# Expert 1 by seven products of halves, and its rows turned while unit 0's second layer runs

## The chip, the cores and the metric

The kernel runs on one core of a Trainium2 chip. The metric is the time of one execution in microseconds (us) of device time; a profiled execution has, beside its own time, a span from the first instruction to the last.

## What is computed

A linear attention over 4 batches, 8 heads and 576 positions feeds a dense block of three input matrices with a maximum over them, and this feeds a layer of eight experts, of which each of the 2304 tokens uses two. Cut to what matters here:

```
def _moe_ref(x, w1, w2, w3, w_out):
    h = np.maximum(np.maximum(x @ w1, x @ w2), x @ w3)
    return h @ w_out                                   # 512 -> 768 -> 512

def _moe2_ref(x, w_gate, w_noise, noise, w1, w2):
    noisy_logits = x @ w_gate + np.log1p(np.exp(x @ w_noise)) * noise
    top2 = np.argpartition(-noisy_logits, 2, axis=1)[:, :2]
    ...
    for e in range(E):                                 # 8 experts, 512 -> 1024 -> 512
        for k in range(2):
            mask = top2[:, k] == e
            h = np.maximum(x[mask] @ w1[e], 0.0)
            out[mask] += top2_w[mask, k, None] * (h @ w2[e])
```

Inputs and outputs are float32.

## The kernel before

Every float32 matrix is split into a high part in the matmul's own format and the low rest (`split`: an ACT copy and a DVE subtraction), and a product is three matmuls: high by high, high by low, low by high. The program is one list of steps with planned times (`at`, `pe`, `after`); sorted by these times it is the order on PE, ACT, DVE and SP. POOL's DMAs and additions keep the order of the list too where `in_order` stands. Each engine works through its own instructions in order, and so does SP's queue of DMAs.

After the attention (some 180 us) the dense block works through six chunks of 384 tokens (`first`, `larger`, `hidden`, `second`). While it runs, DVE, ACT, POOL and SP do side work: the routing of finished chunks, which scatters each token's row into a table `meta` in DRAM by its expert, and the sum jobs (`quarter_load`, `quarter_sum`, `quarter_high`, `quarter_out`), which prepare sums and differences of quarters of the experts' first matrix and write their high and low parts to `sums`.

Then come the expert units: unit 0 is expert 0 with up to 512 rows, unit 1 the next 128 rows of expert 0, and units 2 to 8 are experts 1 to 7 with up to 608 rows each. In unit 0 and in unit 2 the first layer is done plainly (`expert1`): 8 blocks of hidden features, 4 blocks of input features, 3 matmuls, and for 608 rows two halves of 304 columns, that is 192 matmuls in unit 2. From unit 3 on (`seven(n)`, n > SEVEN = 2) it is done by seven products of halves (`product`, `sum7`, `relu7`, `low7`): seven matrix products of half the size in every direction in place of eight, 168 matmuls of 304 columns, with additions of results on DVE. The operands of the rows, named B11, B21, T1 to T4 and B22, are made by `x_quarters` and `x_sums` from the turned rows; those of the weights are either plain quarters (kind "A") or come from `sums` (kind "S").

The rows of a unit are fetched by token number: `load_meta` loads the table, `gather_x` fetches 128 rows by an indirect DMA of POOL, `turn_x` turns them by four transposes of PE into a PSUM bank t. The second layer (`expert2`, 24 matmuls of 512 columns for 128 rows) ends in `expert_out`: DVE multiplies by the gate and adds the old output that `gather_prev` had read, and an indirect DMA of POOL scatters the result. Unit 1 has its rows as the stationary operand (`tile1`), turns its hidden tile (`tile_turn`) and splits it (`tile_hidden`).

A ring of 12 slots holds weights; slot i+12 is loaded when the weights of slot i have been used (`refill`: `w2_load` by SP into a buffer `raw`, `w2_high` on ACT, `w2_low` on DVE; for kind "S" `w2_high` is two DMAs straight from `sums`). PSUM banks are s0 to s2, t0 and t1, and p0, p1 and k in turn (`bank_acc`).

In unit 0 the turn of unit 1's rows stands ahead of the last of the four tiles of the second layer; the five turns of unit 2's rows stand in unit 1:

```
                if n == 0 and i == len(sizes(M)) - 1:
                    pe(0.45, turn_x, 1, cap_b, 0)
                pe(d2, expert2, n, e, M, i)
```

Of the kernel before, what the change touches and what calls it, by code (L numbers as in the profile page):

```python
# [38 lines left out]
def tile_linear_attention__then__moe__then__noisy_top2_moe(  # L39
# [59 lines left out]
    SEVEN = 2  # L99
# [1001 lines left out]
    def gather_x(n, M, i, nrow, slot=None):  # L1101
        m = sizes(M)[i]
        xgs = st["xgs"]
        if seven(n):
            if len(st["xg7"]) == 1:
                st["xg7"].append(pools["po"].tile([P, DM], F32R, name="xg"))
            xgs, slot = st["xg7"], i % 2
# [6 lines left out]
    def turn_x(n, M, i):  # L1114
# [8 lines left out]
        xh, xl = st["gx"]  # L1123
        cs = slice(i * P, i * P + m)
# [122 lines left out]
    def tile1(n, e, a):  # L1247
        xh, xl = st["gx"]
        p_ = bank_s()
        i = 0  # L1250
        for d in range(KD):
            wh, wl = (w[:, a * HALF2:(a + 1) * HALF2] for w in WE[e, d])
            for l, r in ((xh, wh), (xh, wl), (xl, wh)):
                nc.tensor.matmul(p_, l[:, d, :P], r, start=(i == 0), stop=(i == 3 * KD - 1))
                i += 1
# [342 lines left out]
    def refill(i, n, wait=0.1, rooms=True):  # L1598
        for i in range(i, i + n):
# [4 lines left out]
            if summed(*pairs[i]):  # L1604
                if rooms:
                    after(wait + 1.0 + 3.0 * (i % 4), w2_high, *pairs[i])
                continue
            en, j = pairs[i]
            slow = n_now[0] > 1
            t = max(clock[0] + wait, split_at[-1] + (4.5 if slow else 3.0))  # L1610
            at(max(split_at[-2] + 0.01, t - 9.0), w2_load, en, en, j)
# [66 lines left out]
    for n, (e, M, row0) in enumerate(units):  # L1678
# [35 lines left out]
        else:  # L1714
            for a in range(2):
                pe(2.56, tile1, n, e, a)
                after(0.0, tile_relu, n, a)
# [6 lines left out]
        elif n:  # L1724
            refill(base(e), KD, 3.0 if n == 1 else 0.1)
# [11 lines left out]
        if n == 0:  # L1737
# [3 lines left out]
            at(tp + 17.1, gather_x, 1, cap_b, 0, N + 1, 4)  # L1741
            for i in range(4):
                at(tp + 20.0, gather_x, 2, cap, i, N + 1)
        elif n == 1:
            for i in range(4, nt2):
                at(g0, gather_x, 2, cap, i, N + 1)
        elif nxt:
# [3 lines left out]
        d2 = 3 * F2 * DM / 2400  # L1751
        if M <= P:

            pe(0.45, tile_turn, n, 0)
            after(0.0, tile_hidden, n, 0)
            pe(0.45, turn_x, n + 1, M2, 0)
            pe(0.45, tile_turn, n, 1)
            after(0.0, tile_hidden, n, 1)
            pe(0.45, turn_x, n + 1, M2, 1)
            for a in range(2):  # L1760
                pe(d2 / 2, expert2, n, e, M, 0, range(a * F2 // 2, (a + 1) * F2 // 2))
# [98 lines left out]
```

## Time and profile before

| | |
|---|---|
| median of 3 runs | 944.88 us (944.87 to 945.2) |
| profiled execution: time, span | 945.21 us, 943.7 us |
| PE busy | 930.9 us, 6841 matmuls |
| DVE, ACT, POOL busy | 592.6, 479.0, 512.4 us |
| granted TensorE clock, mean | 0.999 |

The span lies 1.5 us under the execution's own time. Matmuls overlap in their pipeline, so the length of a stretch of PE is read from the start of its first matmul to the start of what follows.

### The profile page before, as it was taken

The page shows a single profiled execution, that of the slowest core. Times are in us where ns is not written, and L with a number is a line of the kernel's source. Part 1 is how long each engine was busy: PE and PEld are TensorE (multiplying, and loading weights), DVE is VectorE, ACT ScalarE, POOL GpSimd, SP SyncE. Part 2 cuts the span into 40 slices and gives each one's busy share as a digit, 9 for nine tenths or more (in the row PEclk, how much of TensorE's full clock was granted, in tenths as well). Part 3 has the DMA queues.
Part 4 walks back from the last instruction along what each step waited for, and adds up shares of the span by engine and source line. Part 5 has one row for each costly group of instructions (what it writes and reads, how often), then busy time and mean ns, then how long its engine had stood idle before and what let it go on. Part 6 is the DMA issues. An engine that isn't in the chain of part 4 may idle for free. (4 is left out here: it accounts for less than half of the span.)

```text
span 943.7 us, 18315 instructions
## 1 busy us (share of the span) xinstructions
PE 930.9 (99%) x6841; PEld 809.3 (86%) x6841; DVE 592.6 (63%) x1251; ACT 479.0 (51%) x1021; POOL 512.4 (54%) x570
## 2 busy tenths in 40 slices
PE   8999999999999999999999999999999999999997
PEld 7777777899999999999997889798987989898895
DVE  6999999895544637363464354566685767657541
ACT  6999998554333333343343243355463735545340
POOL 6888898454474745544243532365564636556262
PEclk9999999999999999999999999999999999999999
DMA  7676653541567566656053646457565757648312
GB/s 196 164 221 178 181 181 108 190 150 59 163 172 235 169 222 178 214 183 206 4 179 112 173 131 259 173 174 276 159 254 173 278 163 235 222 149 310 92 34 73
DMA packets 121580, 164.95 MB, mean 175 GB/s; under 512 B 35438, under 2 KB 83694, under 8 KB 121490
## 3 DMA queue, kind: packets, MB, share of 16 engines
q1 hardware_dynamic: 110002, 133.83, 45.2%
q0 software_dynamic: 10928, 29.62, 9.2%
q8 instruction: 54, 0.88, 0.4%
q10 hardware_dynamic: 560, 0.33, 0.1%
q14 instruction: 36, 0.29, 0.1%
HBM read 117.28 MB, written 47.05 MB: 174 GB/s over the span
## 5 line engine op out<-in xcount | busy, mean ns | idle before, releaser
L886 PE MATMUL s<-xh,wh 128*128 128x384 f32 x432 | 148.1, 343 | 0.4 <-ACT wh L276 0.4
L886 PE MATMUL s<-xh,wl 128*128 128x384 f32 x432 | 145.4, 337 | 0.4 <-DVE wl L278 0.4
L886 PE MATMUL s<-xl,wh 128*128 128x384 f32 x432 | 145.1, 336 | 0.0
L1332 POOL DMA_INDIRECT out_dram<-o,emeta x40 | 46.8, 1170 | 125.4 <-DVE o L1330 66.5
L1407 DVE TENSOR_TENSOR wl<-raw,wh 128x1024 fp32r<-128x1024 f32 x58 | 71.2, 1227 | 30.0 <-ACT wh L1399 29.5
L896 DVE TENSOR_TENSOR a<-s,a 128x384 f32<-128x384 f32 x72 | 39.9, 554 | 77.4 <-PE s L886 76.7
L886 PEld LDWEIGHTS s<-xh,wh 128*128 128x128 f32 x432 | 81.2, 188 | 6.6 <-DVE a L896 2.2
L1322 PE MATMUL p<-wh,hh 128*128 128x512 f32 (+1 forms) x216 | 86.4, 400 | 0.0
L1322 PE MATMUL p<-wh,hl 128*128 128x512 f32 (+1 forms) x216 | 85.4, 395 | 0.0
L1322 PE MATMUL p<-wl,hh 128*128 128x512 f32 (+1 forms) x216 | 85.2, 395 | 0.0
L886 PEld LDWEIGHTS s<-xl,wh 128*128 128x128 f32 x432 | 81.2, 188 | 1.5
L886 PEld LDWEIGHTS s<-xh,wl 128*128 128x128 f32 x432 | 81.1, 188 | 0.7 <-DVE wl L278 0.7
L1399 ACT ACTIVATE wh<-raw 128x1024 fp32r<-128x1024 f32 x58 | 61.1, 1056 | 34.0 <-DMA raw<-in_moe_w_dram 19.3
L1047 POOL DMA_INDIRECT meta<-mt,si x36 | 37.0, 1028 | 52.8 <-DVE si L1043 43.6
L1375 POOL TENSOR_TENSOR raw<-raw 128x256 f32<-128x256 f32 x24 | 21.7, 903 | 75.1 <-DMA raw<-in_moe_w_dram 51.8
L1180 PE MATMUL s<-gx,wh 128*128 128x304 f32 x288 | 62.1, 303 | 0.0
L243 POOL TENSOR_TENSOR nm<-nm,bits 128x512 int32<-128x512 int32 (+1 forms) x32 | 38.3, 1206 | 42.0 <-DVE nm L233 26.1
L131 ACT ACTIVATE hh<-a 128x384 fp32r<-128x384 f32 x36 | 18.8, 522 | 80.7 <-DVE a L896 80.7
L132 DVE TENSOR_TENSOR gx<-t,gx 128x512 fp32r<-128x512 f32 (+3 forms) x82 | 39.5, 496 | 30.7 <-ACT gx L131 30.5
L131 ACT ACTIVATE gx<-t 128x512 fp32r<-128x512 f32 (+3 forms) x82 | 34.9, 448 | 42.7 <-DVE t L1155 27.4
L1109 POOL DMA_INDIRECT gx<-x2d,emeta x28 | 28.7, 1023 | 41.5 <-PE t L1119 17.1
L1330 DVE SCALAR_TENSOR_TENSOR o<-p,emeta,pv 128x512 f32<-128x512 f32 (+1 forms) x27 | 20.2, 749 | 47.3 <-PE p L1322 41.3
(318 smaller groups left out, 2642.4 us busy)
## 6 DMA issues: line engine op xcount, KB each, us to landing
raw<-in_moe_w_dram SPq DMA_DIRECT2D x58, 512.0 KB, 4.4
raw<-in_moe_w_dram SPq DMA_DIRECT2D x48, 256.0 KB, 4.0
sums<-qh SPq DMA_DIRECT2D x24, 512.0 KB, 3.0
sums<-raw SPq DMA_DIRECT2D x24, 512.0 KB, 3.4
wh<-sums SPq DMA_DIRECT2D x24, 512.0 KB, 6.1
wl<-sums SPq DMA_DIRECT2D x24, 512.0 KB, 7.0
bits<-in_moe_w_dram SPq DMA_DIRECT2D x18, 512.0 KB, 5.7
out_dram<-zrow SPq DMA_DIRECT2D x9, 512.0 KB, 3.9
```

The lines of the kernel that those rows point to most:

```text
L131: nc.scalar.activation(hi, src, AF.Copy)
L132: nc.vector.tensor_tensor(lo, src, hi.bitcast(F32), op=ALU.subtract)
L243: in_order(nc.gpsimd.tensor_tensor(m_[:, i:i + w], m_[:, i:i + w], low[:, i:i + w], op=ALU.add))
L886: nc.tensor.matmul(p_, a[:, d, fs], b_, start=(n == 0), stop=(n == 3 * KD - 1))
L896: nc.vector.tensor_tensor(a, p_, st.pop("a"), op=ALU.max)
L1047: ins = nc.gpsimd.indirect_dma_start(out=meta, out_offset=bass.IndirectOffsetOnAxis(ap=si[:, t, kk:kk + 1], axis=0), in_=mt[:, t, kk, :], ...
L1109: in_order(nc.gpsimd.indirect_dma_start(out=xg.bitcast(F32)[:m], out_offset=None, in_=x2d[0:nrow, :], in_offset=bass.IndirectOffsetOnAxis( ...
L1180: nc.tensor.matmul(bk["p"], a[:, d, fs], b_[:, d, :], start=(d == 0 and i == 0), stop=(d == 1 and i == 2))
L1322: nc.tensor.matmul(p_, a, b_[:, fw], start=(f == 0 and r == 0), stop=(f == (3 if seven(n) else F2 - 1) and r == 2))
L1332: alone(e, nc.gpsimd.indirect_dma_start(out=out, out_offset=bass.IndirectOffsetOnAxis(ap=mt[:m, i, 1:2], axis=0), in_=o[:m], in_offset=Non ...
L1399: nc.scalar.activation(WE[e, i][0], st["w2", e, i], AF.Copy)
L1407: nc.vector.tensor_tensor(wl, st.pop(("w2", e, i)), wh.bitcast(F32), op=ALU.subtract)
```

## The change

`SEVEN` becomes 1, so unit 2 (expert 1) has its first layer by seven products too, and four more sum jobs (28 in place of 24) prepare its weights, at a pitch of 7.4 planned us and not 8.0. The buffers of the gathered rows of unit 2 are then two in turn (one in the big tile, called gx in a row, one of its own, called xg), and unit 1's rows come through the second of them. Since the operands of unit 2 lie in the big tile, unit 1's operands `x1` move to two of the three buffers named pv, and its hidden tile `th` to the buffers of `o`. The turns of unit 2's rows move: the first stands ahead of the third tile of unit 0's second layer together with unit 1's turn, the second ahead of the fourth tile, the third and fourth behind it, the fifth in unit 1. In unit 1 `tile1` is cut, `tile_turn` put between its pieces, and the second layer is begun ahead of the second `tile_turn`. Times of `refill` and places of `gather_prev` change with it.

```diff
-    SEVEN = 2
+    SEVEN = 1
...
     def gather_x(n, M, i, nrow, slot=None):
...
-        if seven(n):
-            if len(st["xg7"]) == 1:
-                st["xg7"].append(pools["po"].tile([P, DM], F32R, name="xg"))
-            xgs, slot = st["xg7"], i % 2
+        if n == 1:
+            st["xg7"].append(pools["po"].tile([P, DM], F32R, name="xg"))
+        if n == 1 or seven(n):
+            xgs, slot = st["xg7"], i % 2 if seven(n) else 1
...
         xh, xl = st["gx"]
+        if n == 1:
+            st["x1"] = xh, xl = tuple(pools["po"].tile([P, KD, P], F32R, name="x1", tag="pv", bufs=3)
+                                      for _ in range(2))
...
-        h = pools["po"].tile([P, HALF2], F32, name="th", tag="pv", bufs=3)
+        h = pools["po"].tile([P, HALF2], F32, name="th", tag="o", bufs=2)
...
-                t = clock[0] + 8.0 * i
+                t = clock[0] + 7.4 * i
...
-            for a in range(2):
-                pe(2.56, tile1, n, e, a)
-                after(0.0, tile_relu, n, a)
+            pe(2.56, tile1, n, e, 0)
+            after(0.0, tile_relu, n, 0)
+            pe(1.28, tile1, n, e, 1, range(2))
+            pe(0.45, tile_turn, n, 0)
+            after(0.0, tile_hidden, n, 0)
+            pe(1.28, tile1, n, e, 1, range(2, KD))
+            after(0.0, tile_relu, n, 1)
+            after(0.01, gather_prev, 1, 0, cap_b, 0)
...
-            refill(base(e), KD, 3.0 if n == 1 else 0.1)
+            refill(base(e), KD - 1, 1.9)
...
+            pe(0.7 * 2, expert2, n, e, M, 0, range(2))
             pe(0.45, tile_turn, n, 1)
             after(0.0, tile_hidden, n, 1)
...
+            turns7(4)
+            rows7(2)
+            pe(0.7 * 2, expert2, n, e, M, 0, range(2, 4))
+            pe(d2 / 2, expert2, n, e, M, 0, range(4, F2))
             after(0.0, expert_out, n, e, M, 0)
...
-                if n == 0 and i == len(sizes(M)) - 1:
+                if n == 0 and i == 2:
                     pe(0.45, turn_x, 1, cap_b, 0)
+                    after(0.02, gather_x, 2, cap, 1, N + 1)
+                    turns7(0, 1)
+                if n == 0 and i == 3:
+                    turns7(1, 1)
+                    rows7(0)
                 pe(d2, expert2, n, e, M, i)
...
+                if n == 0 and i == 2:
+                    after(0.0, gather_prev, n, e, M, 3)
...
+        if n == 0:
+            turns7(2, 1)
+            turns7(3, 1)
+            rows7(1, 2.6)
```

On POOL, in unit 0's second layer, before: the three table loads (unit 1, unit 2 and its rest) are followed by five gathers and then by the outputs (`out_dram`) of unit 0's tiles and the reads of old output (`pv`).

```order
L1076 DMA emeta<-meta 128x3
L1076 DMA emeta<-meta 128x4x3
L1080 DMA emeta<-meta 96x3
L1109 DMA gx<-x2d,emeta 128x512 x5
L1332 DMA out_dram<-o,emeta 2304x512
L1294 TENSOR_SCALAR ic<-emeta 128x1
L1297 DMA pv<-out_dram,ic 128x512
```

With the change, from the third table load to unit 0's last output; the first xg is unit 1's gather, the others are unit 2's rows 0 to 3 in turn (gx, xg, gx, xg).

```order
L1080 DMA emeta<-meta 96x3
L1109 DMA xg<-x2d,emeta 128x512
L1109 DMA gx<-x2d,emeta 128x512
L1334 DMA out_dram<-o,emeta 2304x512 x2
L1109 DMA xg<-x2d,emeta 128x512
L1109 DMA gx<-x2d,emeta 128x512
L1334 DMA out_dram<-o,emeta 2304x512
L1296 TENSOR_SCALAR ic<-emeta 128x1
L1299 DMA pv<-out_dram,ic 128x512
L1109 DMA xg<-x2d,emeta 128x512
L1334 DMA out_dram<-o,emeta 2304x512
```

Two gathers stay ahead of the outputs, and the gather of unit 2's fourth tile (the last xg) now stands behind unit 0's third output, the index clamp and the read of the fourth tile's old output.

On PE, with the change, the end of unit 0's second tile and the start of its third (bank k):

```order
L1324 MATMUL p_6898<-wh,hl_6847 128x512
L1119 MATMUL t_6928<-exact,xg 128x128 x4
L1119 MATMUL t_6937<-exact,gx 128x128 x4
L1324 MATMUL k<-wh,hh_6598 128x512
L1324 MATMUL k<-wl,hh_6598 128x512
```

Two turns, of unit 1's rows and of unit 2's first tile, now stand here; before, PE went from the second tile to the third directly, and unit 1's turn stood ahead of the fourth.

On DVE, with the change, at the end of unit 1 and the start of expert 1: the last row pieces of unit 2 (48 columns, t_7131), a weight split (wl), unit 1's output (o from bank k) and the first additions of the seven products.

```order
L132 TENSOR_TENSOR gx<-t_7131,gx 128x4x48
L132 TENSOR_TENSOR gx<-t_7131,gx 128x2x48
L1409 TENSOR_TENSOR wl<-raw,wh 128x1024
L1158 TENSOR_TENSOR t_7131<-b_7145,t_7131 128x2x48
...
L1158 TENSOR_TENSOR t_7131<-t_7131,b_7146 128x2x48
L132 TENSOR_TENSOR gx<-t_7131,gx 128x2x48
L132 TENSOR_TENSOR gx<-b_7146,gx 128x2x48
L132 TENSOR_TENSOR gx<-t_7131,gx 128x4x48
L1332 SCALAR_TENSOR_TENSOR o<-k,emeta,pv 128x512
L1409 TENSOR_TENSOR wl<-raw,wh 128x1024
L1202 TENSOR_TENSOR u<-s_7219,t 128x304
L1202 TENSOR_TENSOR u<-k,t 128x304
```

Unit 1's output is read out of bank k behind all the row pieces, and bank k is used again by the second product of expert 1 (u from k).

## Rows read from the trace of the kernel before

**Rows 1.** The page's table of engines: busy time, share of the span, instructions.

```profile
PE 930.9 (99%) x6841; PEld 809.3 (86%) x6841; DVE 592.6 (63%) x1251; ACT 479.0 (51%) x1021; POOL 512.4 (54%) x570
```

**Rows 2.** PE busy in two stretches: first layers of experts 1 and 2.

```profile
558.69:585.65 26.96, 26.96 (x194) 1.00 0.63 224
615.28:638.83 23.55, 23.55 (x170) 1.00 0.61 203
```

**Rows 3.** Timeline of PE: start, length, instruction, idle time before it and releaser.

```profile
657.45 0.49 PE L1119 MATMUL t<-exact,gx 96*128 96x96 f32 x4 [0.20 <-DMA gx<-x2d,emeta]
...
713.45 0.49 PE L1119 MATMUL t<-exact,gx 96*128 96x96 f32 x4 [1.23 <-DMA gx<-x2d,emeta]
...
873.81 0.49 PE L1119 MATMUL t<-exact,gx 96*128 96x96 f32 x4 [0.41 <-DMA gx<-x2d,emeta]
```

**Rows 4.** Busy time of each engine from 244 to 486 us, the dense stage.

```profile
sum 242.00, PE 242.00 PEld 226.40 DVE 119.94 ACT 88.48 POOL 119.31; mean PE 48.40 PEld 45.28 DVE 23.99 ACT 17.70 POOL 23.86
```

**Rows 5.** The same from 522 to 559 us: unit 0's second layer, unit 1.

```profile
sum 37.00, PE 37.00 PEld 30.05 DVE 14.46 ACT 10.33 POOL 14.80; mean PE 18.50 PEld 15.02 DVE 7.23 ACT 5.17 POOL 7.40
```

**Rows 6.** The sum jobs' split: duration in ns (least/median/most), first and last start.

```profile
L1384 ACT ACTIVATE qh<-raw x24: 1044/1053/1065, 237.0 to 437.5; 128x1024 fp32r<-128x1024 f32 x24
...
L1389 DVE TENSOR_TENSOR raw<-raw,qh x24: 1210/1227/1762, 239.2 to 438.5; 128x1024 fp32r<-128x1024 f32 x24
```

**Rows 7.** Timeline of PE, three tiles of second layers and two turns.

```profile
533.24 0.40 PE L1322 MATMUL k<-wh,hh 128*128 128x512 f32 x1
...
538.85 0.45 PE L1119 MATMUL t<-exact,gx 128*128 128x128 f32 x4
539.13 0.47 PE L1322 MATMUL p<-wh,hh 128*128 128x512 f32 x1
...
604.13 0.48 PE L1322 MATMUL p<-wh,hh 128*128 128x512 f32 x1
```

**Rows 8.** Timeline of POOL in unit 0's second layer: table loads, two gathers.

```profile
525.44 1.38 POOL L1076 DMA_DIRECT2D emeta<-meta  x2 [3.60 <-DMA meta<-mt,si]
...
530.36 1.02 POOL L1109 DMA_INDIRECT gx<-x2d,emeta  x1 [3.00 <-DMA emeta<-meta]
531.69 1.53 POOL L1109 DMA_INDIRECT gx<-x2d,emeta  x1 [0.30 <-issue]
```

**Rows 9.** Landing times of the five gathers from 530.36, then of the second.

```profile
DMA to landing us min/median/max: 3.6/4.1/5.3
...
DMA to landing us min/median/max: 5.3/5.3/5.3
```

**Rows 10.** Timeline of SP's queue, 522 to 536 us: loads of weights.

```profile
522.32 3.08 SPq L1349 DMA_DIRECT2D raw<-in_moe_w_dram  x2
529.60 3.18 SPq L1346 DMA_DIRECT2D raw<-in_moe_w_dram  x2
```

**Rows 11.** Landing time of the gather issued at 550.23.

```profile
DMA to landing us min/median/max: 3.2/3.2/3.2
```

**Rows 12.** Landing time of the table load issued at 525.44.

```profile
DMA to landing us min/median/max: 4.6/4.6/4.6
```

**Rows 13.** Timeline of DVE: two outputs and a last low part.

```profile
533.44 0.75 DVE L1330 SCALAR_TENSOR_TENSOR o<-p,emeta,pv 128x512 f32<-128x512 f32 x1 [1.08 <-PE p L1322]
...
608.13 0.36 DVE L132 TENSOR_TENSOR gx<-t,gx 128x192 fp32r<-128x192 f32 x1 [0.23 <-ACT gx L131]
609.97 0.75 DVE L1330 SCALAR_TENSOR_TENSOR o<-p,emeta,pv 128x512 f32<-128x512 f32 x1 [1.48 <-PE p L1322]
```

**Rows 14.** Timeline of POOL: outputs, read of old output, gather.

```profile
594.65 1.03 POOL L1332 DMA_INDIRECT out_dram<-o,emeta  x1 [5.35 <-DVE o L1330]
...
596.25 1.05 POOL L1297 DMA_INDIRECT pv<-out_dram,ic  x1 [0.28 <-POOL ic L1294]
...
611.00 0.99 POOL L1332 DMA_INDIRECT out_dram<-o,emeta  x1 [3.74 <-DVE o L1330]
...
709.45 0.94 POOL L1109 DMA_INDIRECT gx<-x2d,emeta  x1 [0.30 <-issue]
```

More of the change, by code (lines that the diff above doesn't have):

```diff
@@ L1245, in tile_linear_attention__then__moe__then__noisy_top2_moe, with tile1 @@
     HALF2 = FF2 // 2
[L1247 to L1251, printed above, removed]
+    def tile1(n, e, a, ds_=range(KD)):
+        xh, xl = st["x1"] if n == 1 else st["gx"]
+        p_ = st["tp", n, a] if ds_[0] else bank_s()
+        for d in ds_:
             wh, wl = (w[:, a * HALF2:(a + 1) * HALF2] for w in WE[e, d])
-            for l, r in ((xh, wh), (xh, wl), (xl, wh)):
-                nc.tensor.matmul(p_, l[:, d, :P], r, start=(i == 0), stop=(i == 3 * KD - 1))
-                i += 1
+            for i, (l, r) in enumerate(((xh, wh), (xh, wl), (xl, wh))):
+                nc.tensor.matmul(p_, l[:, d, :P], r, start=(d == 0 and i == 0),
+                                 stop=(d == KD - 1 and i == 2))
         st["tp", n, a] = p_
     def tile_relu(n, a):
-        h = pools["po"].tile([P, HALF2], F32, name="th", tag="pv", bufs=3)
+        h = pools["po"].tile([P, HALF2], F32, name="th", tag="o", bufs=2)
         nc.scalar.activation(h, st.pop(("tp", n, a)), AF.Relu)
@@ L1605, in refill @@
                 if rooms:
-                    after(wait + 1.0 + 3.0 * (i % 4), w2_high, *pairs[i])
+                    after(0.3 + 0.6 * (i % 4) if n_now[0] == 1 else wait + 1.0 + 3.0 * (i % 4), w2_high, *pairs[i])
                 continue
             en, j = pairs[i]
-            slow = n_now[0] > 1
+            slow = n_now[0] > 0
             t = max(clock[0] + wait, split_at[-1] + (4.5 if slow else 3.0))
-            at(max(split_at[-2] + 0.01, t - 9.0), w2_load, en, en, j)
+            at(max(split_at[-2] + 0.01, t - (4.0 if n_now[0] == 1 else 9.0)), w2_load, en, en, j)
             at(t, w2_high, en, j)
@@ L1740, in tile_linear_attention__then__moe__then__noisy_top2_moe @@
                 at(tp + 17.0, load_meta, n_, row_, M_, 0)
[L1741 to L1747, printed above, removed]
+            at(tp + 17.1, gather_x, 1, cap_b, 0, N + 1)
+            at(tp + 20.0, gather_x, 2, cap, 0, N + 1)
+        elif n > 1 and nxt:
             at(g0 + 2.0, load_meta, n + 1, row2, M2, 0)
@@ L1751, in tile_linear_attention__then__moe__then__noisy_top2_moe, with turns7, rows7 @@
         d2 = 3 * F2 * DM / 2400
+        def turns7(i, n=n):
+            pe(0.45, turn_x, n + 1, cap, i)
+            if i + 2 < len(sizes(cap)):
+                after(0.02, gather_x, n + 1, cap, i + 2, N + 1)
+        def rows7(j, wait=1.6):
+            after(0.5, x_quarters, j)
+            after(wait, x_sums, j)
         if M <= P:
[L1754 to L1756 removed]
+            pe(0.7 * 2, expert2, n, e, M, 0, range(2))
             pe(0.45, tile_turn, n, 1)
             after(0.0, tile_hidden, n, 1)
[L1759 to L1763 removed]
+            turns7(4)
+            rows7(2)
+            pe(0.7 * 2, expert2, n, e, M, 0, range(2, 4))
+            pe(d2 / 2, expert2, n, e, M, 0, range(4, F2))
             after(0.0, expert_out, n, e, M, 0)
[L1765 to L1775 removed]
+        else:
             if nxt and n > 0:
@@ L1799, in tile_linear_attention__then__moe__then__noisy_top2_moe @@
                         rows7(2)
+        if n == 0:
+            turns7(2, 1)
+            turns7(3, 1)
+            rows7(1, 2.6)
         if n:
-            refill(base(e) + (len(ORDER7) if seven(n) else KD), F2 // 2, 15.0 if n == 1 else 0.1)
+            if seven(n):
+                refill(base(e) + len(ORDER7), F2 // 2)
+            else:
+                refill(base(e) + KD - 1, F2 // 2 + 1, 0.3)
     ET = mybir.EngineType
```

19 lines of the change are left out of this document (3 added, 16 removed).

## The prediction

> **What bounds the kernel now.** I read the page's table of engines first. PE is busy 930.9 of 943.7 us [rows 1], so only two things can move the time: fewer TensorE instructions, or new waits of TensorE. Then I cut the second part of the trace into stretches. The first layer of expert 1, by twelve products per output block, takes 26.96 us of PE without a gap. The first layer of expert 2, by seven products of halves, takes 23.55 us [rows 2]. The second half of the program is a chain of such stretches with few holes. Where there are holes, most stand ahead of the fifth turn of gathered rows, which waits for an indirect DMA: 0.20, 1.23 and 0.41 us [rows 3]. In the dense stage the wide jobs run under a PE that is busy 242.00 of 242.00 us [rows 4]. Unit 0's second layer and unit 1 run without a hole as well, 37.00 of 37.00 us [rows 5]. So gain and loss have to be read at two places: the first layer of expert 1, and the 37 us ahead of it, where the change puts turns that need fresh gathers.
>
> **The saving.** Expert 1 goes from 192 matmuls of 304 columns to 168, the count that experts 2 to 7 have (the counts in the rows, 194 and 170, take in a neighbour or two). By [rows 2] that is 26.96 - 23.55 = 3.4 us. The matmuls of unit 1, of both second layers and the six turns are the same in number as before, only elsewhere. I take that part as even.
>
> **Four more sum jobs in the dense stage.** Each has four POOL additions, one ACT copy of 1.05 us, one DVE subtraction of 1.23 us [rows 6] and its loads and stores; 28 jobs at a pitch of 7.4 instead of 24 at 8.0. DVE is busy 119.94, ACT 88.48 and POOL 119.31 of 242 us there [rows 4], four jobs add about 5 us to DVE and 4 to ACT. PE waits for nothing in this stage, and what hides the jobs is the PE's own work. I cost them at nothing. If a job's subtraction came straight before an evacuation that PE needs, it would cost at most its 1.2 us, once.
>
> **First wait: rows of units 1 and 2 in unit 0's second layer.** The turn of unit 1's rows stood after the third tile (at 538.85) and now stands after the second, with the first turn of expert 1 behind it. PE is there at 533.24 [rows 7]. The gathers can't come sooner than POOL lets them: the landing of the last routing scatter releases the table loads at 525.44, and the landing of the first table releases the first gather at 530.36; the second starts at 531.69 [rows 8]. The change touches neither. In before the five gathers from there took 3.6 to 5.3 us from issue to landing, the second one 5.3 [rows 9], so it landed at 537.0. The new turn of expert 1's first tile is wanted at 533.24 + 0.28 = 533.5. If nothing gets quicker, PE waits 537.1 - 533.5 = 3.6 us. But in before two loads of 512 KB were issued from 529.60 on, in this very stretch [rows 10], and these now wait for slots of unit 1. A gather in a quiet stretch landed after 3.2 us [rows 11]; the table load took 4.6 us here [rows 12]. If both took 3.2, the first gather would start at 525.44 + 3.2 + 0.3 = 528.9, the second 1.3 later, and land at 533.4: no wait. Between 0 and 3.6 I take 1.0, nearer to the quiet end, since the later loads are gone but those from 522.32 on are partly still there when the table is read.
>
> **Second wait: the fourth tile of expert 1.** This one hangs on an order and less on the state of the DMAs. Its gather stands on POOL behind unit 0's third scatter, an index clamp and the read of old output, and that scatter needs the third tile's result. Counted from the end of that tile on PE: 0.2 until DVE starts (533.24 to 533.44), 0.75 for the result, 0.28 until POOL starts (610.72 to 611.00) [rows 13, 14]; from scatter to read 1.6, the read 1.05, 0.3 between DMAs [rows 14]: 4.2 us until the gather is issued. Then 3.2 (quiet) to 5.3 us to the landing, and 0.1: 7.5 to 9.6. PE gets to the fourth turn after one turn, one tile and another turn: 0.28 + 5.6 + 0.28 = 6.2 us (a tile is 533.24 to 538.85, a turn 538.85 to 539.13) [rows 7]. So the wait is 1.3 to 3.4 us, wherever the first wait put the tile. No load of SP stands there, so I take 1.5. The same kind of chain is seen in before: the gather of 709.45 [rows 14] ends in the hole of 1.23 us.
>
> The Trainium skill, in "DMA: Bandwidth & Descriptors", section "Anatomy of one DMA — SWDGE (gpsimd) path", gives a DMA of POOL's queue about 2.0 us plus its bytes over 436 GB/s. For a gather of 256 KB that is 2.6 us, an estimate from that section of the Trainium skill, and each of the two waits would be about 0.6 us shorter by it. The rows say otherwise: none of the six gathers of [rows 9, 11] landed in less than 3.2 us.
>
> **Third wait: bank k at the start of expert 1.** The last piece of expert 1's operands (48 columns) is now made some 7 us ahead of its use, and unit 1's output comes behind it on DVE: two low parts, a weight split, four subtractions, three low parts, and only then the output from bank k. From the end of a fifth turn (604.13) [rows 7] to the last of these low parts (608.49) the same pieces took 4.4 us. A weight split on ACT and DVE, of the shapes of [rows 6], adds 1.1 and 1.15, the output 0.75 [rows 13]: 7.4 us. PE has three quarters of a tile (4.2) and three products (3 x 0.85, from 23.55 / 28) until it writes bank k again, 6.75 us. So 0.6 us of wait with the release; 0 to 1.2, as the weight split falls.
>
> **Others.** Expert 1's own fifth turn becomes one of those that wait for a gather with POOL's low parts in its queue. Of the five experts that do so in before, the one that makes the overflow table waited 1.23 us, the others 0.20, 0.41 and twice nothing: 0.1. The transposes of unit 1's hidden tile wait for an ACT step that is now among the row pieces; the second half of the tile, 1.4 us, covers it, and I give it nothing (0.5 if the cover is short). Weights of expert 1's last three products are loaded when unit 1 frees their slots, and are wanted some 14 us later; nothing, unless half-megabyte loads take three times the 4.6 us of [rows 12].
>
> **Sum.** -3.4 + 1.0 + 1.5 + 0.6 + 0.1 = -0.2 us. The profiled execution took 945.21 us, 0.3 over the median of 944.88; from the median that is 944.7. With every wait at its low end it is -3.4 + 1.3 = -2.1; with every wait at its high end -3.4 + 3.6 + 3.4 + 1.2 + 0.5 + 0.4 = +5.7.
>
> **Rivals.** A measurement tells a difference of about 0.2%, 1.9 us, from no change.
> - *The waits all but vanish (faster).* The first gather lands in time, the fourth tile's wait is at its 1.3 us or below, the third is covered: 944.88 - 2.1 to - 3.4, or 941.5 to 942.8. For it speaks that SP is idle there now; against it, that the second wait is an order of instructions. With what lies between it and 943.0 I give it 0.28. By the gather time of the Trainium skill's "DMA: Bandwidth & Descriptors" it would nearly be this case: waits of 0.4, 0.9, 0.6 and 0.1, 943.5.
> - *The turns are too early for the gathers (slower).* Table load and gathers need what they needed in before, 4.6 and 5.3 us; the first wait is 3.6 and the second 3.4. With the rest that is +4.3, or 949.2. It decides from 5.3 us of waits in all. Against it: the loads that shared the DMAs are gone. 0.12.
> - *The sum jobs show on PE (slower).* With the waits above, two subtractions of 1.2 us in front of evacuations that PE needs are enough: -0.2 + 2.4, or 947.1. PE shows no hole with 24 jobs. 0.03.
>
> The forecast, saving and waits cancelling to within 1.9 us, has 0.57.
>
> **How the numbers follow.** Forecast 944.7 us. Faster 0.28, same 0.57 and slower 0.15 come straight from the cases. The range leaves out a good tenth below, where the waits come to less than 0.8 us in all (942.3), and the slower cases above, where they come to more than 5.3 (946.8).
>
> **What would show it.** The first layer of expert 1 in some 23.5 us of PE. A hole of PE ahead of the turn of expert 1's first rows, released by the gather, of 0 to 3.6 us; one ahead of its fourth tile of 1.3 us or more; one of half a microsecond at the second pair of products, released by DVE's output from bank k. No hole in the dense stage. The prediction is wrong if the fourth tile's turn doesn't wait, or if holes of over 5 us stand between unit 0's second tile and expert 1's second layer.

## The result: 953.6 us, slower by 0.9%

The changed kernel takes 953.57 us (median of 6 runs, 951.97 to 955.6) where the kernel before takes 945.04 beside it (6 runs, 944.87 to 946.2): a ratio of 1.009, 95% interval 1.0075 to 1.0105. The forecast was 944.7 with a range up to 946.8, so the time lies outside it, 8.9 us above the forecast. The profiled execution took 955.29 us with a span of 953.4, against a span of 943.7 before. Where times of a few us are told below, it helps to know that single executions of one kernel lie up to 3.8 us from their median, and that the kernel before gave medians of 945.0 to 945.8 in the comparisons of this study. One execution of e1_jobs_only below took 1214.09 us at a mean granted clock of 0.704 and is in no median here.

### The profile page after: what moved, and what is told of

Read it like the earlier page. It is cut to its first block, busy times and chain, and to the rows that moved or that the text cites. A ratio compares the mean times of both kernels' runs of the same rounds, so it can differ in the third digit from the quotient of the medians.

```text
span 953.4 us, 18474 instructions
## 1 busy us (share of the span) xinstructions
PE 930.7 (98%) x6817; PEld 806.5 (85%) x6817; DVE 614.4 (64%) x1292; ACT 493.9 (52%) x1056; POOL 534.1 (56%) x598
## 5 line engine op out<-in xcount | busy, mean ns | idle before, releaser
L1334 POOL DMA_INDIRECT out_dram<-o,emeta x40 | 48.8, 1220 | 127.4 <-DVE o L1332 73.0
L1409 DVE TENSOR_TENSOR wl<-raw,wh 128x1024 fp32r<-128x1024 f32 x57 | 77.2, 1354 | 20.8 <-ACT wh L1401 15.9
L1324 PE MATMUL p<-wh,hh 128*128 128x512 f32 (+1 forms) x208 | 82.9, 399 | 0.0
L1324 PE MATMUL p<-wh,hl 128*128 128x512 f32 (+1 forms) x208 | 82.4, 396 | 0.0
L1324 PE MATMUL p<-wl,hh 128*128 128x512 f32 (+1 forms) x208 | 82.1, 395 | 0.0
L1377 POOL TENSOR_TENSOR raw<-raw 128x256 f32<-128x256 f32 x28 | 23.1, 825 | 90.5 <-DMA raw<-in_moe_w_dram 70.9
L1183 PE MATMUL s<-gx,wh 128*128 128x304 f32 x336 | 72.5, 302 | 0.0
L1047 POOL DMA_INDIRECT meta<-mt,si x36 | 38.7, 1074 | 32.6 <-DVE si L1043 23.3
L1183 PEld LDWEIGHTS s<-gx,wh 128*128 128x128 f32 x336 | 55.6, 189 | 0.7
L1183 PE MATMUL s<-gx,wl 128*128 128x304 f32 x168 | 50.9, 303 | 0.0
```

Of the source, the lines that this page charges most:

```text
L1047: ins = nc.gpsimd.indirect_dma_start(out=meta, out_offset=bass.IndirectOffsetOnAxis(ap=si[:, t, kk:kk + 1], axis=0), in_=mt[:, t, kk, :], ...
L1183: nc.tensor.matmul(bk["p"], a[:, d, fs], b_[:, d, :], start=(d == 0 and i == 0), stop=(d == 1 and i == 2))
L1324: nc.tensor.matmul(p_, a, b_[:, fw], start=(f == 0 and r == 0), stop=(f == (3 if seven(n) else F2 - 1) and r == 2))
L1334: alone(e, nc.gpsimd.indirect_dma_start(out=out, out_offset=bass.IndirectOffsetOnAxis(ap=mt[:m, i, 1:2], axis=0), in_=o[:m], in_offset=Non ...
L1377: ins = nc.gpsimd.tensor_tensor(a22, a21, a22, op=ALU.add)
L1409: nc.vector.tensor_tensor(wl, st.pop(("w2", e, i)), wh.bitcast(F32), op=ALU.subtract)
```

## The profile after

The page's table of engines of the changed kernel (as [rows 1]):

```profile
PE 930.7 (98%) x6817; PEld 806.5 (85%) x6817; DVE 614.4 (64%) x1292; ACT 493.9 (52%) x1056; POOL 534.1 (56%) x598
```

PE does 24 instructions fewer in a span that is 9.7 us longer: what was added is waiting. The dense stage, which had not a gap in [rows 4], is the first place. Windows view, 244 to 486 us, the sums of the engines:

```profile
sum 242.00, PE 239.23 PEld 222.87 DVE 121.96 ACT 91.55 POOL 125.88; mean PE 239.23 PEld 222.87 DVE 121.96 ACT 91.55 POOL 125.88
```

The waits of PE in the changed kernel, from its timeline (start, length, instruction, idle time before it and what ended it), in the dense stage and then in the experts 1 and 2:

```profile
335.56 0.50 PE L913 MATMUL p<-wh,hh 128*128 128x512 f32 x1 [1.13 <-ACT hh L131]
...
444.60 0.50 PE L913 MATMUL p<-wh,hh 128*128 128x512 f32 x1 [1.59 <-ACT hh L131]
...
551.68 0.50 PE L1119 MATMUL t<-exact,xg 128*128 128x128 f32 x4 [1.36 <-DMA xg<-x2d,emeta]
...
567.31 0.55 PE L1183 MATMUL k<-gx,wh 128*128 128x304 f32 x2 [0.20 <-DVE o L1332]
...
582.62 0.55 PE L1183 MATMUL p<-gx,wh 128*128 128x304 f32 x2 [1.58 <-DVE t L1202]
...
610.35 0.49 PE L1119 MATMUL t<-exact,gx 96*128 96x96 f32 x4 [1.31 <-DMA gx<-x2d,emeta]
...
639.06 0.41 PE L1183 MATMUL k<-gx,wh 128*128 128x304 f32 x1 [1.01 <-DVE t L1202]
...
666.34 0.49 PE L1119 MATMUL t<-exact,gx 96*128 96x96 f32 x4 [1.31 <-DMA gx<-x2d,emeta]
```

In the dense stage the loss is larger than its two waits: set beside the same blocks of before, the two rows stand for 3.70 us. PE's blocks are 0.69 us later than in before until 332, 2.40 from 338 and 4.38 from 447. The wait of 1.36 is the predicted one for the fourth tile, that of 0.20 the predicted one for bank k. The four after it, 5.2 us together, are not in the prediction.

**The dense stage.** Timeline of POOL in the changed kernel ahead of the first of these waits. L1377 is the first of the four additions of a sum job, L1382 the last; L1047 are the six routing scatters of a chunk:

```profile
316.91 0.74 POOL L1377 TENSOR_TENSOR raw<-raw 128x256 f32<-128x256 f32 x1 [9.07 <-DMA raw<-in_moe_w_dram]
...
320.25 1.01 POOL L1047 DMA_INDIRECT meta<-mt,si  x1 [0.15 <-issue]
...
327.44 0.96 POOL L1047 DMA_INDIRECT meta<-mt,si  x1 [0.30 <-issue]
328.43 0.74 POOL L1377 TENSOR_TENSOR raw<-raw 128x256 f32<-128x256 f32 x1
...
330.88 0.74 POOL L1382 TENSOR_TENSOR raw<-raw 128x256 f32<-128x256 f32 x1
```

And what ACT and DVE did there (timelines of these engines):

```profile
331.66 1.06 ACT L1386 ACTIVATE qh<-raw 128x1024 fp32r<-128x1024 f32 x1 [5.01 <-POOL raw L1382]
334.98 0.52 ACT L131 ACTIVATE hh<-a 128x384 fp32r<-128x384 f32 x1 [2.26 <-DVE a L896]
...
332.75 1.73 DVE L1391 TENSOR_TENSOR raw<-raw,qh 128x1024 fp32r<-128x1024 f32 x1 [3.95 <-ACT qh L1386]
334.40 0.55 DVE L896 TENSOR_TENSOR a<-s,a 128x384 f32<-128x384 f32 x1
```

The scatters of the same chunk in the kernel before (its timeline of POOL), and the second such place in the changed kernel:

```profile
312.88 1.01 POOL L1047 DMA_INDIRECT meta<-mt,si  x1 [1.56 <-DVE si L1043]
```

```profile
419.90 0.74 POOL L1377 TENSOR_TENSOR raw<-raw 128x256 f32<-128x256 f32 x1 [6.43 <-DMA raw<-in_moe_w_dram]
```

Read from the top: POOL waits 9.07 us, in order, for the load of a sum job, with the scatters queued behind it. In before the scatters start at 312.88, since there this sum stands behind them; here they start at 320.25. So the next sum ends at 331.6. ACT stands at that job's copy for 5.01 us, DVE at its subtraction for 3.95, and the maximum `a` that PE's next block needs is queued behind them on DVE, `hh` behind that on ACT.

**The experts.** Timelines of POOL and of DVE in the changed kernel around the wait of 1.58. `hl` is the low part that POOL computes, `wl` that of a weight, which takes DVE 1.21 to 1.23 us when nothing is in its way:

```profile
574.67 1.03 POOL L1109 DMA_INDIRECT gx<-x2d,emeta  x1 [3.94 <-PE s L1183]
576.00 0.97 POOL L1109 DMA_INDIRECT xg<-x2d,emeta  x1 [0.30 <-PE s L1183]
576.99 1.70 POOL L1221 TENSOR_TENSOR hl<-v,hh 128x304 fp32r<-128x304 f32 x2
578.61 1.67 POOL L1221 TENSOR_TENSOR hl<-u,hh 128x304 fp32r<-128x304 f32 x2
580.23 0.85 POOL L1221 TENSOR_TENSOR hl<-t,hh 128x304 fp32r<-128x304 f32 x1
...
577.70 4.48 DVE L1409 TENSOR_TENSOR wl<-raw,wh 128x1024 fp32r<-128x1024 f32 x1 [1.19 <-ACT wh L1401]
582.10 0.46 DVE L1202 TENSOR_TENSOR t<-p,t 128x304 f32<-128x304 f32 x1
```

The split ends at 582.18, 1.10 us after POOL's last subtraction of the run (581.08), about the time that it takes alone: it seems to have stood still while they ran. Behind it stands the addition (`t` from bank p) that reads the bank which PE's next product writes, and PE waits for that. Splits of 3.91 us at 634.71 and 2.96 at 691.07 fall into such runs as well; the first of them ends 1.09 us after its run, the second gets in ahead of its run's last member. In before the longest split took 1.60 us. The Trainium skill, "SBUF — State Buffer", section "SBUF: two separate sides", says that a VectorE operation with two SBUF inputs and a GpSimd operation that reads SBUF share a port pair which one of them holds for its whole instruction, the other fully blocked. By that page of the Trainium skill one subtraction of 0.85 us would hold the split; the rows show a hold by five, and the measurement decides.

## The experiments

Every time is a median beside runs of the kernel before on the same chip, with the ratio to them.

**e1_jobs_only: the sum jobs alone, in the kernel before.**

```diff
-    sums = tc.dram_tile([E - SEVEN, 4, 2, P, 2, FF2 // 2], F32, name="sums")
+    sums = tc.dram_tile([E - SEVEN + 1, 4, 2, P, 2, FF2 // 2], F32, name="sums")
...
-    jobs = [(e, a, c) for e in range(SEVEN, E) for a in range(2) for c in range(2)]
+    jobs = [(e, a, c) for e in range(SEVEN - 1, E) for a in range(2) for c in range(2)]
...
-                t = clock[0] + 8.0 * i
+                t = clock[0] + 7.4 * i
```

> The kernel before with one part of the change alone: four more sum jobs in the dense stage, 28 at a pitch of 7.4 us where there were 24 at 8.0. Expert 1 is computed as before with all its products, so the four sums that the new jobs store are not used. Theory (the loss of 4.4 us in the dense stage comes from these jobs): about 949.3 us, 4.4 above before, with two PE waits on ACT's hh in the dense stage (near 335 and 445 us) that before lacks. Rival (the jobs are covered, as the prediction had it, and the dense loss has another source in the change): 944.9 to 945.2 us, no such wait.

Measured: 950.02 us (7 executions), ratio 1.0049 (1.0033 to 1.0064), 4.7 us more than the 945.3 beside it. Its PE timeline has the two waits, and no new ones in the experts:

```profile
336.21 0.50 PE L913 MATMUL p<-wh,hh 128*128 128x512 f32 x1 [1.45 <-ACT hh L131]
...
446.92 0.50 PE L913 MATMUL p<-wh,hh 128*128 128x512 f32 x1 [1.73 <-ACT hh L131]
```

So the part that the prediction costed at nothing loses, by itself, more than half of the 8.5 us.

**e2_pitch8: the changed kernel at the old pitch.**

```diff
-                t = clock[0] + 7.4 * i
+                t = clock[0] + 8.0 * i
```

> The changed kernel with its 28 sum jobs at the old pitch of 8.0 us, nothing else. Theory (the pitch decides: at 7.4 us two jobs come behind the routing scatters on POOL, whose late sums hold up ACT and DVE): the dense stage ends 4.4 us earlier and the time is about 949 us, with the waits of the experts 1 to 3 as they are. Rival one (the number of jobs decides, each costing about 1 us wherever it stands): 953 to 954 us. Rival two (at 8.0 us the last job reaches past the dense stage into the shared expert or unit 0, and costs there what it saved): between the two.

Measured: 964.09 us, ratio 1.0184 (1.0163 to 1.0204), 10.5 us above the changed kernel. No theory had this size. The two waits in the dense stage near 335 and 445 us are gone; where the last jobs now meet the weight splits for the experts, at the dense stage's end, there are two far longer ones:

```profile
492.39 0.69 PE L886 MATMUL s<-xh,wh 128*128 128x384 f32 x1 [5.91 <-DVE a L896]
...
507.23 0.62 PE L1119 MATMUL t<-exact,gx 128*128 128x128 f32 x3 [5.62 <-DVE gx L132]
```

DVE stands there in order at weight splits whose loads come late, and the maxima PE waits for stand behind. So 28 jobs cost more at 8.0 than at 7.4, each pitch with a collision of its own; no pitch between them was tried.

**e3_late: the next expert's two early gathers behind POOL's first six subtractions.**

```diff
-                at(g0 + 2.1, gather_x, n + 1, M2, i, N + 1)
+                at(g0 + 11.9, gather_x, n + 1, M2, i, N + 1)
```

> The changed kernel with the two early gathers of the next expert's rows issued 9.8 us later in each of the units 2 and up, so that on POOL the first six hl subtractions stand ahead of these gathers and not behind. Theory (DVE's wl splits of 4.48, 3.91 and 2.96 us are held by POOL's hl subtractions, which run back to back because the gathers ahead of them wait for the table load): for the experts 2 and 3 the long splits fall to about 1.2 us, the PE waits on t of 1.01 and 0.28 us go, and with them parts of the later waits; between 948.5 and 951.5 us. The 4.48 us split in expert 1's stage may stay, where the order of unit 1 is as it was. Rival (the splits are long since weights or sums come late, POOL's neighbourhood has nothing to do with it): splits as long as now, 953 to 954 us. A loss is possible if the gathers, now later, hold up the first turns of the next expert.

Measured: 963.25 us, ratio 1.0186 (1.016 to 1.0211). The mechanism came out as expected: no split of experts 1 to 3 takes over 1.4 us and the three waits on `t` (1.58, 1.01, 0.28) are gone. The time came out as the loss that was named as possible: the gathers are late for the second turn in six experts, as here by 2.65 us:

```profile
648.85 0.60 PE L1119 MATMUL t<-exact,xg 128*128 128x128 f32 x3 [2.65 <-DMA xg<-x2d,emeta]
```

**e4_first: the fourth tile's gather ahead of unit 0's third output on POOL.**

```diff
-                after(0.95 if nxt and n and i == 1 else -0.01, expert_out, n, e, M, i)
+                after(0.95 if nxt and n and i == 1 else 0.48 if n == 0 and i == 2 else -0.01, expert_out, n, e, M, i)
...
-                    after(0.0, gather_prev, n, e, M, 3)
+                    after(0.49, gather_prev, n, e, M, 3)
```

> The changed kernel with the gather of expert 1's fourth tile put ahead of unit 0's third output store, its ic and pv on POOL, where the change has it behind them. Theory (the 1.36 us wait for that gather in unit 0's second layer is the order on POOL): the wait goes; 952.0 to 952.4 us if what follows keeps its offsets, 953.6 if a later wait takes it up. Rival (the gather lands late by its own transfer, not by its place): the wait stays, 953.6 us.

Measured: 948.11 us, ratio 1.0029 (1.0016 to 1.0042): 5.5 us less than the changed kernel for a wait of 1.36. The wait is gone, and with it the waits on `t`; the splits of experts 1 to 3 take at most 2.07 us, and the fifth turns wait 0.17 and 0.37 instead of 1.31 twice. The expectation had the place right and missed that the later waits would go with it; whether they hang on it alone is seen from e7_sums and e6_first_sums below. Windows view, the whole first layer of expert 1 with the two turns behind it, before (first row) and in e4_first; behind the length stand the busy times of PE, its weight loads, DVE, ACT and POOL:

```profile
558.69:586.29 27.60, 27.60 (x203) 27.60 (x202) 13.15 (x22) 11.45 (x23) 8.27 (x11) 1.00 0.64 228
```

```profile
563.86:588.03 24.17, 24.17 (x177) 24.16 (x176) 18.96 (x40) 15.96 (x33) 15.96 (x19) 1.00 0.76 267
```

With no wait in it the stage is 3.4 us shorter: the saving is what the prediction said.

**e7_sums and e6_first_sums: two sums behind the scatters.** The eleventh and the twenty-fourth sum go behind the scatters that they stood ahead of; e7_sums does this to the changed kernel, e6_first_sums to e4_first.

```diff
-        if (e, a, c) == jobs[0]:
+        if (e, a, c) in (jobs[0], jobs[10], jobs[23]):
...
-                at(t + 5.0, quarter_sum, *job)
+                at(t + {10: 6.5, 23: 7.5}.get(i, 5.0), quarter_sum, *job)
```

> The changed kernel with these two sums behind the scatters, and nothing else. Theory (the dense stage and the gather's place are two losses that add): 3 to 4 us under the changed kernel, 949.5 to 950.5 us, with the waits of the experts 1 to 3 as in the changed kernel. Rival (what the dense stage gives back is lost again behind it, since the experts' waits hang on fixed landings): 953 us.

> The changed kernel with the early gather of the fourth tile (as e4_first, 948.1 us) and with the sums of two jobs, the eleventh and the twenty-fourth, put behind the six routing scatters on POOL that they stand ahead of. Theory (POOL waits 9.07 and 6.43 us for the loads of these two sums while the scatters stand ready behind it; the late scatters make the next sum late, ACT and DVE wait for it in order, and PE for their hh): the two PE waits in the dense stage go, about 3 us with the clock that some of these waits take along; about 944.5 to 945.5 us from 948.1, and down to 942.5 if all that is left of the change is its saving of 3.4 us and some 0.9 us of small waits. Rival (the pitch of 7.4 us is too short for the three buffers wherever the sums stand, so another place waits): 947 to 948 us with a wait elsewhere in the dense stage.

Measured: e7_sums 949.35 us, ratio 1.0042 (1.0027 to 1.0056), 4.2 us under the changed kernel; e6_first_sums 947.16 us, ratio 1.0021 (1.0007 to 1.0036). In both the dense stage runs without a wait, so the order of two sums on POOL is what the loss of 3.7 us hung on. But e6_first_sums gained only 1 us over e4_first, not the 2.6 to 3.6 of its theory: the stages behind had moved, and in the profiled run a split of expert 2 fell into a run of subtractions again, though the fourth tile doesn't wait in it. Its DVE and PE timelines:

```profile
626.85 4.00 DVE L1409 TENSOR_TENSOR wl<-raw,wh 128x1024 fp32r<-128x1024 f32 x1 [1.12 <-ACT wh L1401]
...
631.30 0.55 PE L1183 MATMUL k<-gx,wh 128*128 128x304 f32 x2 [1.10 <-DVE t L1202]
...
659.11 0.49 PE L1119 MATMUL t<-exact,gx 96*128 96x96 f32 x4 [1.82 <-DMA gx<-x2d,emeta]
```

e7_sums shows the other side. Its gain of 4.2 us is a little over the 3 to 4 of its theory, but the theory's second half, that the waits of the experts 1 to 3 stay as they were, was wrong. PE and DVE in e7_sums:

```profile
547.88 0.51 PE L1119 MATMUL t<-exact,xg 128*128 128x128 f32 x4 [1.27 <-DMA xg<-x2d,emeta]
573.88 1.59 DVE L1409 TENSOR_TENSOR wl<-raw,wh 128x1024 fp32r<-128x1024 f32 x1 [1.19 <-ACT wh L1401]
...
682.39 4.01 DVE L1409 TENSOR_TENSOR wl<-raw,wh 128x1024 fp32r<-128x1024 f32 x1 [1.06 <-ACT wh L1401]
686.85 0.55 PE L1183 MATMUL p<-gx,wh 128*128 128x304 f32 x2 [1.33 <-DVE t L1202]
```

The fourth tile waits 1.27 us here, and yet expert 1's split takes 1.59 us and the waits of 1.58 and 1.01 don't come; a split of 4.01 us and a wait of 1.33 come in expert 3 instead. So the fourth tile's wait is neither enough for a long split (e7_sums) nor needed for one (e6_first_sums).

**e10_meta, e13_meta_only, e11_before_meta: the load of the next expert's table 8 us earlier.** The two early gathers wait for this load; now it stands ahead of the last output stores of the expert before. e10_meta is e6_first_sums with it, e13_meta_only the changed kernel, e11_before_meta the kernel before.

```diff
-            at(g0 + 2.0, load_meta, n + 1, row2, M2, 0)
+            at(g0 - 6.0, load_meta, n + 1, row2, M2, 0)
```

> The kernel of e6_first_sums (947.2 us) with the load of the next expert's table issued 8 us earlier on POOL, ahead of the last one or two output stores of the expert before, so that the two gathers that wait for it stand ready right behind those stores. Theory (the hl subtractions run back to back, and hold the port against VectorE's splits, only since the gathers ahead of them wait 4 to 5 us for this load): the gathers start 3 to 5 us earlier in each of the experts 2 to 7, the splits of 2 to 4.5 us fall to 1.2 to 1.8, the waits on t go and those of the fifth turns (1.82 and 1.07 us in the profiled run) shrink; 942.5 to 944.5 us, under the kernel before by 1 to 2.5 us. Rival (the gathers wait for their buffers, not for the table): no change, 946 to 948 us.

> The kernel before with the same earlier table load and nothing else, to tell what that edit is worth without the change. Theory (the edit helps where the POOL work is backlogged, which in the kernel before it hardly is: one split of 1.60 us, fifth-turn waits of 0.20, 1.23 and 0.41 us): 943.5 to 945 us, up to 1.8 us under before. Rival (all of what e10_meta gains it gains here too): 942 us.

> The changed kernel with the earlier table load of e10_meta and nothing else (the two sums ahead of the scatters and the late gather of the fourth tile stay). Theory (the losses of the experts 1 to 3 come through the late gathers and the back-to-back subtractions behind them, whatever made the stage late first): 4.5 to 6 us under the changed kernel, 947.5 to 949 us, without waits on t; the two waits in the dense stage and the 1.36 us wait for the fourth tile stay. Rival (the early table load only pays with the other two edits): 951 to 953.6 us.

Measured: e13_meta_only 946.6 us, ratio 1.0011 (0.9999 to 1.0022), 7.0 us under the changed kernel, though the waits of 1.20, 1.82 and 1.35 us in the dense stage and for the fourth tile are all there; no split of the experts takes over 1.4 us. e10_meta 942.7 us, ratio 0.9969 (0.9957 to 0.9981); e11_before_meta 942.31 us, ratio 0.9966 (0.9952 to 0.998). Timeline of POOL in e10_meta, expert 2:

```profile
615.90 1.70 POOL L1334 DMA_INDIRECT out_dram<-o,emeta  x1 [3.15 <-DVE o L1332]
617.90 1.02 POOL L1109 DMA_INDIRECT gx<-x2d,emeta  x1 [0.30 <-issue]
619.23 0.98 POOL L1109 DMA_INDIRECT xg<-x2d,emeta  x1 [0.30 <-issue]
624.60 0.86 POOL L1221 TENSOR_TENSOR hl<-v,hh 128x304 fp32r<-128x304 f32 x1 [4.40 <-ACT hh L1212]
```

The gathers follow the output at once, and POOL then waits for its operands where it had a backlog: the subtractions are 4.4 us of idle time away from the gathers. In the changed kernel's profile the gather of 574.67 has PE named as what ended its wait of 3.94 us; that the wait goes with the earlier load shows that the load held it. Both kernels beat the kernel before. The theory for e11_before_meta, that the edit gains at most 1.8 us there, was wrong: it gains 3.1. With all three edits the change is worth nothing that these runs can tell: 942.7 against 942.3.

**e8_lock, e9_lock2, e12_lock3, e14_lock4: the split and the subtractions by themselves.** Small kernels that compute nothing of the reference. Their core, in the last form:

```diff
+                nc.gpsimd.tensor_tensor(t, (v if i else go)[:, :304], hh[:, :304], op=ALU.subtract)
+                if i == 0 and kind in ("gather", "same"):
+                    nc.gpsimd.indirect_dma_start(
+                        out=next(freshx), out_offset=None, in_=x2d[0:N, :],
+                        in_offset=bass.IndirectOffsetOnAxis(ap=idx[:, 0:1], axis=0))
...
+                nc.vector.tensor_tensor(wl, a, b, op=ALU.subtract)
```

> A kernel by itself that computes nothing of the reference (its output is zeros): a VectorE subtraction of two SBUF tiles, 128x1024, four times alone and then once into chains of 1, 2, 3, 5, 7 and 8 GpSimd subtractions of 128x304 that stand back to back; then a VectorE copy of one SBUF tile of that size, and a subtraction of 128x512 that reads one input from PSUM, into chains of 7. Theory (the 4.48 us split is an exclusive hold of a shared port, kept by GpSimd over its whole back-to-back run): 1.2 us alone; into the chains about 1.2 us plus what is left of the chain, so up to some 6 us with 8 subtractions of 0.85 us; the subtraction with one PSUM input as long as it would be alone. Rival one (the two share the port by turns): the split grows by no more than twice, whatever the chain's length. Rival two (the long splits come from something else in the large kernel): 1.2 us in every chain.

> The kernel of e8_lock (nothing of the reference, zeros out), but each GpSimd subtraction now writes a tile of its own, so that none of a chain after its first waits for a semaphore: chains of 1, 3, 5 and 7 with one VectorE subtraction of two SBUF tiles (128x1024) falling in; then one of 7 in which all but the first write the same tile, so that they wait for each other as in e8_lock; then 7 without waits with a VectorE copy of one SBUF tile, with a subtraction that reads PSUM, and with the two-tile subtraction again. Theory (GpSimd keeps the port as long as its next instruction is ready, and lets go where it waits for a semaphore): about 1.2 us plus the rest of the chain in the chains without waits, some 2.7, 4.3 and 5.9 us for chains of 3, 5 and 7, and 1.6 us in the chain with waits, as in e8_lock. Rival (GpSimd gives way after each instruction in any case, and what held the splits of the large kernel is something else, as the gathers ahead of the chain): 1.6 us everywhere.

> A kernel by itself (nothing of the reference, zeros out), after e8_lock and e9_lock2 showed that chains alone hold a split no longer than 1.6 us. Five chains of 7 GpSimd subtractions, each with one VectorE split of 128x1024 falling in, which come nearer to the large kernel by steps: float32 as in e9_lock2; outputs in float32r on both engines, as there; the same while ScalarE copies 128x1024 tiles; the same with an indirect gather issued between the first and the second subtraction; float32 without ScalarE, with the gather. Theory (what the large kernel has and e9_lock2 had not is what holds the split): one of the steps brings a split of 4 to 5 us. Rival (the hold needs something that none of these has, or hangs on the phase of the two engines to each other): 1.5 to 1.6 us in all five; then the cause of the hold stays open.

> A kernel by itself (nothing of the reference, zeros out) on what let one of the five splits of e12_lock3 take 4.43 us. Chains of seven GpSimd subtractions of 128x304, the VectorE split of 128x1024 falling in at delays that move by steps of 0.1 to 0.2 us over one subtraction: five without a DMA on GpSimd, six with an indirect gather issued between the first and the second subtraction, two with a plain load issued there, and two with a gather and a chain whose subtractions wait for each other. Theory one (a gather just ahead makes the hold): 1.2 to 1.6 us in all five without a DMA, 4 to 5 us in several of the six with the gather. Theory two (the phase of the split's start within a subtraction decides, with or without a gather): long splits at some delays in both series, at like delays. Rival (chance): no pattern.

Measured: in e8_lock the split takes 1.22 us alone and 1.59 to 1.60 in every chain of two or more, whatever its length; in e9_lock2, with subtractions that wait for nothing, 1.53 to 1.55. Both went against my theory that a ready run holds the port by itself. A subtraction that reads one input from PSUM (128x512) took 0.68 us into a chain of seven in both. In e12_lock3 four splits took 1.5 us and the fifth 4.43: the chain behind a gather. (ScalarE's copies ran earlier than meant there, beside the first two chains.) e14_lock4 then told it apart. DVE's splits there, a chain without a DMA, one behind a gather, one behind a plain load, and one behind a gather whose subtractions wait for each other:

```profile
24.60 1.21 DVE L81 TENSOR_TENSOR wl<-wa,wb 128x1024 f32<-128x1024 f32 x1
...
57.22 4.17 DVE L81 TENSOR_TENSOR wl<-wa,wb 128x1024 f32<-128x1024 f32 x1
...
99.09 3.86 DVE L81 TENSOR_TENSOR wl<-wa,wb 128x1024 f32<-128x1024 f32 x1
...
124.19 1.21 DVE L81 TENSOR_TENSOR wl<-wa,wb 128x1024 f32<-128x1024 f32 x1
```

POOL around the second of these:

```profile
54.59 0.96 POOL L95 DMA_INDIRECT xg<-x2d,idx  x1
55.57 4.73 POOL L93 TENSOR_TENSOR hl<-v,hh 128x304 f32<-128x304 f32 x6
```

The split from 57.22 ends at 61.39, 1.09 us after the chain (60.30), as in the large kernel. All five splits without a DMA take 1.21 to 1.80 us, wherever in a subtraction they start; behind a gather five of six take 3.78 to 4.17, behind a plain load both 3.46 and 3.86; where the subtractions wait for each other, 1.50 and 1.21. The sixth behind a gather took 1.48 us, and so did its like in e12_lock3. In both it was the program's first gather; and in both the split started earliest after the run's first member, 1.23 and 1.22 us, where the held ones started 1.38 to 2.36 us after it. Which of the two made the difference stays open, so the phase of the start is not ruled out behind a gather. Without a DMA no start made a hold: there the splits started 1.16 to 1.82 us into the chain.

## Why the prediction was wrong

- **The saving of 3.4 us: right**, 27.60 to 24.17 in e4_first.
- **"I cost them at nothing" and "at most its 1.2 us, once": the step that failed.** The jobs' busy time was counted against PE's cover. But the covers are queues: a sum job is four steps on four queues, each in order, and two of the 28 sums came to stand ahead of the routing scatters, where POOL waited 9.07 and 6.43 us for their loads. PE lost 3.70 us in the changed kernel's profile, the jobs alone cost 4.7 in e1_jobs_only, and with the two sums behind the scatters (e7_sums) the changed kernel gains 4.2. The rival with the sum jobs (947.1) named the right part and had 0.03. Even the 1.2 us that the prediction's own paragraph allows for the jobs is missing from the high end of its sum: +5.7 should have been +6.9, or 951.8.
- **First wait, 1.0 (0 to 3.6): it was 0**, the low end. The first gather was issued 2.22 us after the first table load (530.07 to 532.29 in the changed kernel), 4.92 in before (525.44 to 530.36). That SP's weight loads no longer share the DMAs there is the prediction's argument; no run tests it.
- **Second wait, 1.5 (1.3 to 3.4): it was 1.36**, by the order on POOL, as e4_first shows.
- **Third wait, 0.6 (0 to 1.2): 0.20**, at bank k, released by DVE's output.
- **"Others", 0.1: the second step that failed.** It took expert 1 for one more expert whose fifth turn waits a little, and gave the stages behind nothing. What the runs showed in its place: the load of the next table and the two gathers behind it come late on POOL, the `hl` subtractions then stand ready right behind the gathers, and a weight split that meets such a run stands until it ends or nearly so, with PE's next bank behind it. Waits of 1.58, 1.31, 1.01 and 1.31 followed. e13_meta_only leaves all the waits ahead of these stages as they are and only brings the gathers earlier: the four waits go and the time falls by 7.0 us, 3.1 of which the early load gives the kernel before too. e4_first took them away as well, by 5.5 us, but e7_sums and e6_first_sums show that the fourth tile's wait doesn't decide it alone. Which split is caught changes when the stages move by a us or so; what share of the 5.5 us that wait has stays open. The two gains overlap and can't be added.

The prediction read each new wait as it would stand by itself. The three that it named came to 1.56 us where it said 3.1, so that by its terms the change would have won. It missed 3.7 us where it saw cover, and some 6.7 (8.5 + 3.4 - 1.56 - 3.7, an estimate that mixes medians with one profiled run) in the experts, of which the four waits above are 5.2. Of its two signs of being wrong neither came: the fourth tile waits, and the holes up to expert 1's second layer come to 3.14 us (1.36, 0.20 and 1.58). What failed lay ahead of that stretch and behind it.

Where the saving goes once the three edits are in is seen in the profiled runs of e10_meta and e11_before_meta. With the change expert 1's first layer is 2.95 us shorter, but 0.5 us are lost ahead of it, its second layer takes 1.46 longer (a fifth-turn wait of 1.07 is in it), and 0.5 go in later stages. The rest, half a us, is less than the medians can tell.

## What to carry to other kernels

A job that fits under a busy engine is free only if none of its steps stands ahead, in some queue's order, of what that engine needs next: for each added step look at what is queued behind it and at the load it waits for, above all on POOL. Small waits that delay a chain of DMA, gather and dependent work on one queue can cost more than their own length, by what they make coincide later. Before a redesign is judged, try the cheap reorderings on the old version too: here an earlier table load gave 3.1 us to the old kernel, nearly the 3.4 that the redesign saves.

## What the hardware showed

A run of GpSimd subtractions behind a DMA that GpSimd had just issued held a VectorE subtraction with two SBUF inputs until the whole run had ended, in seven of eight splits of e14_lock4 (3.46 to 4.17 us for one of 1.22). The same run without a DMA, or one whose members wait for each other, let it through in 1.21 to 1.80 us. The Trainium skill, "SBUF — State Buffer", section "SBUF: two separate sides", gives the hold for one instruction; the runs without a DMA agree (at most 0.6 us more than alone), those behind one don't.

A PE wait can be followed by a lower clock, and so cost more than itself. Windows view of e4_first around its second wait in the dense stage (PE busy, granted clock, DMA share):

```profile
440.00:444.00 4.00, 2.22 (x13) 1.00 0.63 210
444.00:448.00 4.00, 4.00 (x12) 0.62 1.01 319
448.00:452.00 4.00, 4.00 (x26) 0.95 0.96 321
```

After a wait of 1.78 us the granted clock was 0.62 on average over 4 us, so part of that time at the lower level of 1.2 GHz, 12 matmuls instead of some 26: with the next row 4 x 0.38 + 4 x 0.05, about 1.7 us more. The changed kernel's own profiled run had waits of 1.13 and 1.59 us at these places with the clock at 1.00 throughout, so the same place costs more in some profiled runs than in others; why, no run here shows. In e2_pitch8 the clock stood at 0.50, the lower level, in three stretches of 4 us at and behind its long waits.
